# Opening a fused attention and MLP kernel head by head, with row sums in two parts and a fixed order of reciprocals

## The chip, the cores and the metric

One core of one Trainium2 chip. The metric is the device time of one execution in microseconds (us). The kernel before has a median of 1029.04 us over three runs, from 1028.91 to 1029.87.

## What is computed

An attention over 4 batches of 8 heads (576 positions, head size 64), then two MLPs over its 2304 rows. The scores carry a bias made of cumulative sums, which must be ready before the first scores can be formed:

```python
scores = scale * np.matmul(q, k.transpose(0, 1, 3, 2))
cum = np.cumsum(np.maximum(s, 0.0), axis=-1)
bias = -(cum[:, :, :, None] - cum[:, :, None, :])
scores = np.where(causal, -1e9, scores + np.minimum(bias, 0.0))
attn = exp(scores - max); attn = attn / (sum + 1e-9); out = attn @ v
h = x @ w_in;  x = (h * sigmoid(1.702 * h)) @ w_out          # d_model 512, d_ff 2048
h = x @ w2_in; x = (P(h) / Q(h)) @ w2_out                    # P cubic, Q quadratic
```

## The kernel before, in words

**Units.** The attention (`attention`, L401) walks through 16 pairs of heads, four to a batch, and through five blocks of query rows in each pair, in the order 0, 1, 4, 2, 3. So there are 80 units; step j of the loop at L422 forms the scores of unit j, transposes the weights of unit j-3 and multiplies those of unit j-4 by the values. Pair g holds units 5g to 5g+4, and its first scores stand at the start of step 5g.

**Operands of a pair.** Each float32 product is made from rounded high parts and remainders (low parts). `prep` (L170) transposes k and q on TensorE (`main`, L216), writes high parts on ScalarE and low parts on VectorE (`split`, L189), and copies two of them to other partitions (`move`, L227: on GpSimd for pairs 0 and 1, by a DMA on SyncE's queue for the others). Partitions 64 to 67 of the tile `k2` hold the bias: two rows of a sum's high and low part and two rows of ones, so that the matmul itself adds the difference of the sums (`scores_piece`, L248). `bias` (L204) fills these rows: for pair 0 by four DMAs from the sums on the chip (tile `stgA`) and two of ones; for a later pair by one DMA from a DRAM copy, `rows`, which `store_sums` (L112) writes with four DMAs on GpSimd's queue and four on SyncE's. The pair after next is loaded by `pair_load` (L141); k and q have one buffer each (L146), so a fetch of k waits until the transposes of the pair before it have read the buffer.

**Sums.** `sums` (L94) takes the maximum with 0, runs the scan over all 576 positions for all 32 heads, and splits the result into high and low parts.

**A unit's chain.** `unit_scores` (L263) runs per head: two matmuls (L258), a masked minimum on VectorE (L288), exp with a row sum on ScalarE (L295). Then once per unit: 1e-9 is added on GpSimd (L303), VectorE takes the reciprocal (L304), GpSimd scales the weights (L307). The transposes on TensorE (L328, L349) read the scaled weights; `unit_values` (L359) multiplies by v.

**What sets the order.** TensorE's order is the program's own. On the other engines and on the queues a planner orders the instructions within their dependencies. `behind` (L529) adds an edge: what is traced inside it, and runs on the engine of the given instruction, is put after that instruction; it adds no wait on another engine. Weights for the first MLP are loaded (L497, L499) into three slots of `stgA`, whose space the sums use first, and converted by `convert` (L502, on ScalarE, VectorE and GpSimd) at the steps of `CONV_J` (L52), the first at j = 9. Up to step 24 (`cold`) `fill` (L389) puts idle matmuls (L78, `warm`) into TensorE's stream; after it, matmuls of the first MLP.

Of the kernel before, what the change touches and what calls it, by code (L numbers as in the profile page):

```python
# [10 lines left out]
F32 = mybir.dt.float32  # L11
F32R = mybir.dt.float32r
# [3 lines left out]
AF = mybir.ActivationFunctionType  # L16
ALU = mybir.AluOpType
# [9 lines left out]
NP = NH // 2  # L27
NT = NB * S
DM, DF = 512, 2048
P = 128  # L30
# [15 lines left out]
AHEAD = 3  # L46
COPY_V = ((0, 0), (0, 4))
PT_W = (256, 512, 768, 1024)
RUN_ENDS = ((0, 1, 4, 2, 3), (4, 3), (4, 3), (3,))
W2_SLOTS = 7  # L50
LEAD = 2
# [7 lines left out]
class Fused:  # L59
    def __init__(self, tc, q, k, v, s, w1i, w1o, w2i, w2o, a, b, out):  # L60
        self.tc, self.nc = tc, tc.nc
        self.q, self.k, self.v, self.s = q, k, v, s
        self.w = {n: (i.bitcast(I32), o.bitcast(I32)) for n, i, o in ((1, w1i, w1o), (2, w2i, w2o))}
        self.a, self.b, self.out = a, b, out
        self.units = {}
        self.newest = {}


    def consts(self, pool):
# [24 lines left out]
    def sums(self, att):  # L94
        nc = self.nc
        BH = NB * NH
        s32 = self.s32
        nz = att.tile([BH, S], F32, name="nz", tag="bt", bufs=BT_BUFS)
        nc.vector.memset(nz, 0.0)
        self.rows = self.dram.tile([BH // 2, 4, 2, 2, S], F32, name="rows")  # L100
        part = self.stg_slot[:BH, : 6 * S].rearrange("p (i r s) -> p i r s", i=3, r=2)
        self.ones, self.hl = part[:, 0:2].bitcast(F32), part[:, 2]
        for i in range(2):
            nc.gpsimd.memset(self.ones[:, i], 1.0 - 2.0 * i)
        nc.vector.tensor_scalar(s32, s32, 0.0, None, ALU.max)
        cum = att.tile([BH, S], F32, name="cum", tag="bt", bufs=BT_BUFS)
        nc.vector.tensor_tensor_scan(cum, s32, nz, 0.0, ALU.add, ALU.add)
        hi, lo = (self.hl[:, r].bitcast(F32R) for r in range(2))
        nc.scalar.activation(hi, cum, AF.Copy)
        nc.vector.tensor_tensor(lo, cum, hi.bitcast(F32), ALU.subtract)  # L110

    def store_sums(self):  # L112
        nc = self.nc
        for i in range(2):
            for r in (2 * i, 2 * i + 1):
                nc.gpsimd.dma_start(self.rows[:, r, i], self.ones[:16, i])
            for h in range(2):
                nc.sync.dma_start(
                    self.rows[:, 2 - 2 * i : 4 - 2 * i, i, h],
                    self.hl[16 * h : 16 * h + 16].bitcast(F32),  # L120
                )


    def masks(self, att):
# [16 lines left out]
    def pair_load(self, att, b, p, first=False):  # L141
        nc = self.nc
        r = {"v": self.vn[p % 2]}

        for nm, src, eng in (("k", self.k, nc.sync), ("q", self.q, nc.scalar if first else nc.sync)):
            r[nm] = t = att.tile([R6, 2, 6, D], F32, name=f"{nm}n{b}_{p}", tag=f"{nm}n", bufs=1)  # L146
            for h in (slice(0, 1), slice(1, 2)) if first else (slice(0, 2),):
                eng.dma_start(
                    t[:, h].rearrange("i h t d -> i h (t d)"),
                    src[b, 2 * p : 2 * p + 2][h].rearrange("h (i t) d -> i h (t d)", t=6),  # L150
                )

        def values():
            if b == 0 and p < 2:
                nc.gpsimd.memset(r["v"][64:, 4], 0.0)
            if b == 0 and p == 0:
                nc.gpsimd.memset(self.pt4[64:, 512:], 0.0)
# [12 lines left out]
    def prep(self, att, b, p, ld, first=False):  # L170
        nc, ident = self.nc, self.ident
        h0, h1 = slice(0, D), slice(D, P)

        def new(nm, *n):
            return att.tile([P, *n, 2, S], F32R, name=f"{nm}{b}_{p}", tag=nm, bufs=2)

        kh, qs, k2 = new("kh"), new("qs"), new("k2", 2)
        self.pairs[b, p] = {"kh": kh, "qs": qs, "k2": k2, "ld": ld, "O": None}  # L180

        def hi(out, T, scale):
            nc.scalar.activation(out, T, AF.Copy, scale=scale)

        def lo(out, T, h, scale):
            nc.vector.scalar_tensor_tensor(out, T, scale, h.bitcast(F32), ALU.mult, ALU.subtract)


        def split(nm, T, h):  # L189
            T = T.rearrange("p (t i) -> p i t", i=R6)  # L190
            for odd, r in enumerate((h0, h1)):
                t = T[r]

                def cols(x):
                    return x.rearrange("p (i t o) -> p o i t", t=3, o=2)[:, odd]

                if nm == "k":
                    hi(cols(kh[h0, h]), t, 1.0)
                    lo(cols(k2[h0, 0, h]), t, cols(kh[h0, h]), 1.0)
                else:  # L200
                    hi(cols(qs[h0, h]), t, -0.125)
                    lo(cols(qs[h1, h]), t, cols(qs[h0, h]), -0.125)

        def bias():  # L204
            d = k2[D : D + 4].bitcast(F32)
            if not first:
                nc.sync.dma_start(d, self.rows[b * NP + p])
                return
            for i in range(2):
                nc.gpsimd.dma_start(d[2 * i : 2 * i + 2, i], self.ones[:2, i])  # L210
                for h in range(2):
                    nc.sync.dma_start(
                        d[2 - 2 * i : 4 - 2 * i, i, h], self.hl[16 * h : 16 * h + 1].bitcast(F32)
                    )

        def main(nm):  # L216
            for h in range(2):
# [9 lines left out]
        def move(o, i):  # L227
            if b == 0 and p < 2:
                for h in range(2):
                    nc.gpsimd.tensor_copy(o[:, h], i[:, h].bitcast(F32))  # L230
            else:
                nc.sync.dma_start(o.bitcast(F32), i.bitcast(F32))

        bias()
        if first:
            self.warm(4)
        main("k")
        move(kh[h1], kh[h0])
        yield
        if first:  # L240
            self.warm(4)
        main("q")
        move(k2[h0, 1], qs[h0])
        yield

# [17 lines left out]
    def unit_scores(self, att, u, h):  # L263
# [39 lines left out]
        nc.gpsimd.tensor_scalar(inv[:, c], sm[:, c], 1.0e-9, None, ALU.add)  # L303
        rc = nc.vector.reciprocal(inv[:, c], inv[:, c])  # L304
        self.tail = (ex, rc)
        for i, bt in enumerate(bts):
            nc.gpsimd.tensor_scalar(bt[:, :n], bt[:, :n], inv[:, i : i + 1], 1.0, ALU.mult, ALU.mult)  # L307

# [92 lines left out]
    def attention(self, att, mlp):  # L401
        units = [(b, p, t) for b in range(NB) for p in range(NP) for t in (0, 1, 4, 2, 3)]
        n = len(units)
        self.pairs, self.state = {}, {}
# [7 lines left out]
        self.pt4 = att.tile([P, 640], F32, name="pt4", bufs=1)  # L412
        ld = self.pair_load(att, 0, 0, True)
        self.sums(att)
        for _ in self.prep(att, 0, 0, ld, True):
            pass
        start = ld["values"]
        ld = self.pair_load(att, 0, 1)
        start()
        ld["values"]()  # L420
        self.store_sums()
        for j in range(n + AHEAD + 1):  # L422
            i, k = j - AHEAD, j - AHEAD - 1
            tr = iter(())
# [19 lines left out]
            self.fill(q / 3, j < 4)  # L444
            for _ in tr:
                pass
# [509 lines left out]
```

## Time and profile before

| | |
|---|---|
| median of three runs | 1029.04 us |
| the profiled execution: its time / its span | 1032.16 us / 1030.4 us |
| TensorE (PE) busy | 1008.7 us, 98% of the span |
| VectorE (DVE), ScalarE (ACT), GpSimd (POOL) busy | 77%, 70%, 33% |
| DMA read / written | 75.08 MB / 32.05 MB |
| mean granted TensorE clock | 0.993 of full speed |

The profile shows one execution. A row gives the engine, the line in the kernel, the operation, what it wrote and read, and its times. An engine with the letter q (SPq, ACTq, POOLq) is its instruction queue, where DMAs are issued; PEld is the loading of weights into TensorE. Names in the rows are the kernel's tiles: `kn`, `qn` and `vn` are k, q and v as loaded, `tk` and `tq` their transposes, `k` is the tile `k2`, `s` the scores in PSUM (and, on DVE at the start, the loaded s), `cum` the sums, `bt` the weights, `sm` the row sums, `tp` transposed weights, `O` the outputs.

### The profile page before, as it was taken

The numbers are of one execution on the slowest core, as the hardware profiler recorded it, in microseconds if no ns is written. First come the engines' busy times: TensorE is split into PE (matmuls) and PEld (weight loads), VectorE is DVE, ScalarE is ACT, GpSimd is POOL, SyncE is SP. The second block draws the span as 40 slices with busy tenths as digits, with TensorE's granted clock in tenths as the row PEclk, the third lists the DMA queues.
The fourth block names the chain that finished last, engine by engine and source line by source line (L and its number), as shares of the span: only waits on it lengthen the run. The fifth ranks groups of instructions, "written<-read, shape, count | busy, mean of one in ns | idle before, by whom it ended". The sixth has DMA issues, their size and how long they took to land.

```text
span 1030.4 us, 19824 instructions
## 1 busy us (share of the span) xinstructions
PE 1008.7 (98%) x7065; PEld 940.5 (91%) x7074; DVE 797.9 (77%) x1794; ACT 722.7 (70%) x1660; POOL 340.4 (33%) x512
## 2 busy tenths in 40 slices
PE   7999999999999999999999999999999999999997
PEld 4778899999999999999999999899999899999896
DVE  6698767766537977777777847899988989889886
ACT  5799979888756655555555536777877777777765
POOL 6478746644430002322211112222222222222222
PEclk9899999999999999999999999999999999999999
DMA  7366456454218645667657645010010100100000
GB/s 182 91 168 168 106 156 192 123 139 103 56 41 284 194 148 186 214 219 241 235 161 251 203 126 226 1 31 31 1 62 1 32 31 1 62 1 1 32 1 31
DMA packets 79594, 116.71 MB, mean 113 GB/s; under 512 B 25696, under 2 KB 63584, under 8 KB 77900
## 3 DMA queue, kind: packets, MB, share of 16 engines
q1 hardware_dynamic: 73128, 95.96, 31.4%
q0 software_dynamic: 6144, 19.19, 5.2%
q8 instruction: 56, 0.92, 0.4%
q10 hardware_dynamic: 224, 0.30, 0.1%
q14 instruction: 42, 0.34, 0.1%
HBM read 75.08 MB, written 32.05 MB: 104 GB/s over the span
## 4 chain that ended last, share of the span: by engine, by line
PE 89%; DMA 3%; ACT 3%; DVE 2%; issue 1%; POOL 1%; SPq 0%; ACTq 0%; POOLq 0%; DVEq 0%
PE h L585 37%; PE a L762 19%; PE a L609 18%; PE s L258 5%; PE O L374 4%; PE tp L349 3%; DMA raw<-in_moe_w_in_dram 1%; DMA kn<-in_k_dram 1%; ACT bt L295 1%; PE tk L221 1%; PE tp L328 1%; DMA x2p<-st 1%; PE tq L221 0%; DMA raw<-in_moe_w_out_dram 0%; PE idle L78 0%
## 5 line engine op out<-in xcount | busy, mean ns | idle before, releaser
L585 PE MATMUL h<-x,u 128*128 128x288 f32 x1536 | 231.8, 296 | 2.1 <-ACT st L624 1.1
L609 PE MATMUL a<-gh,u 128*128 128x288 f32 x1024 | 231.7, 297 | 0.0
L585 PEld LDWEIGHTS h<-x,u 128*128 128x128 f32 x1536 | 212.9, 188 | 4.5 <-ACT st L624 1.3
L745 POOL TENSOR_TENSOR gl<-u,gh 128x384 fp32r<-128x384 f32 x96 | 105.5, 1099 | 291.4 <-ACT gh L743 245.8
L609 PEld LDWEIGHTS a<-gh,u 128*128 128x128 f32 x1024 | 172.9, 188 | 1.4 <-issue 0.5
L585 PE MATMUL h<-y,u 128*128 128x384 f32 x864 | 165.7, 336 | 0.0
L585 PEld LDWEIGHTS h<-y,u 128*128 128x128 f32 x864 | 152.9, 188 | 6.2
L609 PE MATMUL a<-gl,u 128*128 128x288 f32 x512 | 150.0, 294 | 0.3 <-DVE gl L602 0.3
L762 PE MATMUL a<-u,gh 128*128 128x512 f32 x432 | 114.6, 394 | 0.9 <-ACT gh L743 0.9
L596 ACT ACTIVATE g<-h 128x288 f32<-128x288 f32 x128 | 52.2, 408 | 83.0 <-PE h L585 82.1
L671 POOL DMA_DIRECT2D x<-xp x64 | 35.3, 553 | 206.2 <-DVE g L597 89.4
L295 ACT ACTIVATE bt<-bt,mn 128x128 f32<-128x128 f32 (+2 forms) x144 | 83.6, 582 | 19.9 <-DVE mn L288 17.8
L609 PEld LDWEIGHTS a<-gl,u 128*128 128x128 f32 x512 | 96.5, 188 | 1.1 <-DVE gl L602 0.6
L762 PEld LDWEIGHTS a<-u,gh 128*128 128x128 f32 x432 | 80.0, 188 | 14.9 <-ACT gh L743 1.8
L288 DVE CUSTOM_DVE_ANT_0 bt<-s,mask 128x128 f32<-128x128 f32 (+2 forms) x144 | 69.2, 482 | 30.6 <-PE s L258 28.2
L307 POOL TENSOR_SCALAR bt<-bt,sm 128x128 f32<-128x128 f32 (+2 forms) x144 | 81.6, 577 | 29.0 <-DVE sm L304 20.7
L743 ACT ACTIVATE gh<-u 128x384 fp32r<-128x384 f32 x96 | 50.6, 527 | 55.0 <-DVE u L741 53.1
L599 ACT ACTIVATE gh<-g 128x288 fp32r<-128x288 f32 x128 | 56.4, 442 | 43.0 <-DVE g L597 41.5
L597 DVE SCALAR_TENSOR_TENSOR g<-g,h 128x288 f32<-128x288 f32 x128 | 57.5, 450 | 32.5 <-ACT g L596 31.4
L728 ACT ACTIVATE y<-h,cf 128x384 f32<-128x384 f32 x96 | 55.5, 578 | 37.6 <-PE h L585 37.6
L258 PE MATMUL s<-k 68*128 68x256 f32 (+2 forms) x192 | 72.4, 382 | 4.3 <-DMA k<-stgA 3.8
L733 DVE SCALAR_TENSOR_TENSOR y<-s,cf,y 128x384 f32<-128x384 f32 x96 | 59.3, 618 | 21.7 <-ACT s L730 20.7
(109 smaller groups left out, 2071.9 us busy)
## 6 DMA issues: line engine op xcount, KB each, us to landing
raw<-in_moe_w_in_dram SPq DMA_DIRECT2D x24, 512.0 KB
raw<-in_moe_w_out_dram SPq DMA_DIRECT2D x24, 512.0 KB
x<-xp POOLq DMA_DIRECT2D x64, 144.0 KB, 2.9
wd<-park POOLq DMA_DIRECT2D x36, 256.0 KB, 3.8
u<-wd SPq DMA_DIRECT2D x8, 1024.0 KB
x2p<-st SPq DMA_DIRECT2D x32, 144.0 KB
xp<-x2p SPq DMA_DIRECT2D x32, 144.0 KB
xp<-x SPq DMA_DIRECT2D x32, 144.0 KB
```

What stands on the lines that cost most here:

```text
L258: nc.tensor.matmul(sc[: c1 - c0, :w], lhsT=q[:, c0:c1], rhs=k[:, j0 : j0 + w], start=m == 0, stop=m == 1,)
L288: nc.vector.tensor_tensor_reduce(bt[:, j0 : j0 + w], sc[:, :w], mask, 1.0, 3.0e38 if i == 0 else mn[:, 0:1], ALU.add, ALU.min, mn[:, i : i ...
L295: ex = nc.scalar.activation(bt[:, :n], bt[:, :n], AF.Exp, bias=mn[:, i : i + 1], scale=-1.0, accum_out=sm[:, col : col + 1],)
L307: nc.gpsimd.tensor_scalar(bt[:, :n], bt[:, :n], inv[:, i : i + 1], 1.0, ALU.mult, ALU.mult)
L585: nc.tensor.matmul(ps_tile, lhsT=u[:, wl, kk * P : (kk + 1) * P], rhs=x(xl, kk), start=(n == 0), stop=(n == 3 * KD - 1),)
L597: nc.vector.scalar_tensor_tensor(g[:, :w], g[:, :w], 1.0, h, ALU.add, ALU.mult)
L599: self.newest["act"] = nc.scalar.activation(gh[:, :w], g[:, :w], AF.Copy)
L609: nc.tensor.matmul(acc, lhsT=u[:, wl, d * P : (d + 1) * P], rhs=g[gl], start=(first and i == 0), stop=(last and i == 2),)
L728: nc.scalar.activation(y, h, AF.Abs, scale=cf[:, 4:5])
L733: nc.vector.scalar_tensor_tensor(y, s, cf[:, 7:8], y, ALU.mult, ALU.add)
L745: nc.gpsimd.tensor_tensor(gl, p, gh.bitcast(F32), ALU.subtract)
L762: nc.tensor.matmul(accs[m], lhsT=g[gl][:, m * P : (m + 1) * P], rhs=u[:, wl, :], start=(f == 0 and i == 0), stop=(f == NF - 1 and i == 2),)
```

## The change

It touches the attention's opening and some orders:

- `sums` works in two parts, positions 0 to 255 and 256 to 575.
- Two lasting tiles take the place of the `k2` tiles allotted per pair. Their partitions 64 to 67 are set to 1 or -1 once, by VectorE for one and GpSimd for the other; later only the rows of sums are overwritten (`sum_rows`). `rows` in DRAM holds the sums alone: two DMAs write it in place of eight, and two in place of one read it per pair.
- Pair 0 is prepared head by head (k and q of head 0, then of head 1), with 8, 7 and 4 idle matmuls in place of 10, 4 and 4. Its rows of sums come by eight DMAs (part, head, kind of row) on SyncE's queue.
- Pair 1's rows come from the sums on the chip by four DMAs on GpSimd's queue, behind the copies of pair 0, not from DRAM.
- Pair 0's values and the store of the sums stand behind pair 0's rows and pair 1's fetch of q on SyncE's queue; pair 1's values are asked for at step 2.
- The loads of weights at the steps of `CONV_J` and `AHEAD_J` stand behind the newest fetch of q on SyncE's queue.
- `split` writes both high parts, then both low parts.
- In batch 0, VectorE's work on the scores of a unit's first head stands behind the reciprocal of the unit two before, that of its second head, and that of `prep`, behind the reciprocal of the unit before (`guard`).

```diff
+PARTS = ((0, 256), (256, 576))
@@ sums
-        self.rows = self.dram.tile([BH // 2, 4, 2, 2, S], F32, name="rows")
-        for i in range(2):
-            nc.gpsimd.memset(self.ones[:, i], 1.0 - 2.0 * i)
-        nc.vector.tensor_scalar(s32, s32, 0.0, None, ALU.max)
-        nc.vector.tensor_tensor_scan(cum, s32, nz, 0.0, ALU.add, ALU.add)
...
+        self.rows = self.dram.tile([BH // 2, 2, 2, S], F32, name="rows")
+        self.hl = self.stg_slot[:BH, 4 * S : 6 * S].rearrange("p (r s) -> p r s", r=2)
+        self.k2 = [att.tile([P, 2, 2, S], F32R, name=f"k2_{i}", bufs=1) for i in range(2)]
+        for k2, eng in zip(self.k2, (nc.vector, nc.gpsimd)):
+            for i in range(2):
+                eng.memset(k2[D : D + 4, i].bitcast(F32), 1.0 - 2.0 * i)
+        for c0, c1 in PARTS:
+            c = slice(c0, c1)
+            with self.behind((scan,) if c0 else ()):
+                nc.vector.tensor_scalar(s32[:, c], s32[:, c], 0.0, None, ALU.max)
+            scan = nc.vector.tensor_tensor_scan(
+                cum[:, c], s32[:, c], nz[:, c], cum[:, c0 - 1 : c0] if c0 else 0.0, ALU.add, ALU.add
+            )
+            hi, lo = (self.hl[:, r, c].bitcast(F32R) for r in range(2))
+            nc.scalar.activation(hi, cum[:, c], AF.Copy)
+            nc.vector.tensor_tensor(lo, cum[:, c], hi.bitcast(F32), ALU.subtract)
+    def store_sums(self):
+        for h in range(2):
+            self.nc.sync.dma_start(self.rows[:, :, h], self.hl[16 * h : 16 * h + 16].bitcast(F32))
+    def sum_rows(self, g, src, eng, h=slice(0, 2), c=slice(0, S)):
+        d = self.k2[g % 2][D : D + 4].bitcast(F32)
+        for i in range(2):
+            self.rows_in = eng.dma_start(d[2 - 2 * i : 4 - 2 * i, i, h, c], src)
@@ prep
+            for t, o in zip((T[h0], T[h1]), cols(high)):
+                hi(o, t, scale)
+            for t, o, i in zip((T[h0], T[h1]), cols(low), cols(high)):
+                lo(o, t, i, scale)
...
+            for h in range(2):
+                with self.behind(tuple(self.parts) if h else ()):
+                    main("k", (h,))
+                    main("q", (h,))
+                move(kh[h1], kh[h0], (h,))
+                move(k2[h0, 1], qs[h0], (h,))
+                self.warm(4 if h else 7)
+            return
+        if g > 1:
+            self.sum_rows(g, self.rows[g], nc.sync)
@@ unit_scores
+        self.guard = (rc,) if b == 0 else (), self.guard[0]
@@ attention
-        self.warm(10)
+        self.warm(8)
...
+        for c0, c1 in PARTS:
+            for h in range(2):
+                self.sum_rows(0, self.hl[16 * h : 16 * h + 1, :, c0:c1].bitcast(F32), nc.sync,
+                              h, slice(c0, c1))
+        rows = self.rows_in
...
+        with self.behind((self.moved,)):
+            for h in range(2):
+                self.sum_rows(1, self.hl[16 * h + 1 : 16 * h + 2].bitcast(F32), nc.gpsimd, h)
+        with self.behind((rows, self.fetched)):
+            start()
+            self.store_sums()
+        later.append(ld["values"])
...
-                self.unit_scores(att, units[j], 0)
+                with self.behind(self.guard[1]):
+                    self.unit_scores(att, units[j], 0)
                 if j:
-                    next(nprep, None)
+                    with self.behind(self.guard[0]):
+                        next(nprep, None)
+                if j == 2:
+                    with self.behind((rows, self.fetched)):
+                        later.pop(0)()
...
-                self.unit_scores(att, units[j], 1)
+                with self.behind(self.guard[0]):
+                    self.unit_scores(att, units[j], 1)
...
             if j in CONV_J or j in AHEAD_J:
-                with self.behind(self.tail):
+                with self.behind((*self.tail, self.fetched)):
                     self.emit(1)
```

## Rows read from the trace of the kernel before

**Rows 1.** The page: the span in 40 equal slices, in tenths.
```profile
PE   7999999999999999999999999999999999999997
PEclk9899999999999999999999999999999999999999
```

**Rows 2.** Windows by pair: length; PE, PEld, DVE, ACT, POOL busy; clock, DMA share, GB/s.
```profile
12.00:25.15 13.15, 10.79 (x58) 7.73 (x60) 8.53 (x32) 8.76 (x25) 6.15 (x15) 0.87 0.80 222
25.15:43.50 18.35, 17.09 (x126) 13.60 (x126) 10.91 (x40) 11.79 (x33) 6.23 (x15) 0.72 0.34 83
43.50:58.00 14.50, 13.23 (x127) 10.30 (x127) 12.71 (x45) 13.99 (x40) 9.24 (x16) 1.00 0.53 143
58.00:72.00 14.00, 13.72 (x126) 10.48 (x129) 12.38 (x44) 13.74 (x40) 11.21 (x18) 1.00 0.71 180
```

**Rows 3.** The chain of waits, 0 to 30 us: start, length, what.
```profile
4.00 0.46 DVE s L105
4.49 1.36 DVE cum L107
5.87 0.69 ACT stgA L109
6.58 0.75 DVE stgA L110
...
8.80 3.06 DMA k<-stgA
...
16.97 9.52 DMA kn<-in_k_dram
```

**Rows 4.** The timeline of SyncE's queue, 0 to 30 us: start, length, what.
```profile
7.36 2.62 SPq L212 DMA_DIRECT2D k<-stgA  x4
10.08 0.36 SPq L148 DMA_DIRECT2D kn<-in_k_dram  x1
...
11.40 1.95 SPq L118 DMA_DIRECT2D rows<-stgA  x4
13.53 0.39 SPq L497 DMA_DIRECT2D stgA<-in_moe_w_in_dram  x1
...
15.99 0.93 SPq L497 DMA_DIRECT2D stgA<-in_moe_w_in_dram  x2
16.97 0.50 SPq L148 DMA_DIRECT2D kn<-in_k_dram  x1
```

**Rows 5.** The timeline of TensorE, 0 to 46 us, with the idle time before.
```profile
11.99 0.55 PE L258 MATMUL s<-k 68*128 68x256 f32 x1 [3.81 <-DMA k<-stgA]
...
14.74 0.95 PE L221 MATMUL tk<-ident,kn 96*128 96x96 f32 x6
...
23.48 0.89 PE L349 MATMUL tp<-ident,bt 128*128 128x128 f32 x4 [2.34 <-POOL bt L307]
...
25.15 0.39 PE L258 MATMUL s<-k 68*128 68x256 f32 x1
...
26.63 1.19 PE L221 MATMUL tk<-ident,kn 96*128 96x96 f32 x6 [0.97 <-DMA kn<-in_k_dram]
...
43.54 0.39 PE L258 MATMUL s<-k 68*128 68x256 f32 x1
```

**Rows 6.** The timeline of GpSimd, 0 to 52 us: start, length, what.
```profile
8.55 0.99 POOL L116 DMA_DIRECT2D rows<-stgA  x2
...
10.92 1.27 POOL L230 CAST k<-qs 64x576 fp32r<-64x576 f32 x2
...
18.63 0.22 POOL L303 TENSOR_SCALAR sm<-sm 128x2 f32<-128x2 f32 x1
...
22.95 0.94 POOL L307 TENSOR_SCALAR bt<-bt,sm 128x256 f32<-128x256 f32 x2 [1.47 <-DVE sm L304]
...
49.04 1.30 POOL L515 TENSOR_TENSOR stgA<-stgA 128x512 int32<-128x512 int32 x1
```

**Rows 7.** The timeline of VectorE, 20 to 52 us: start, length, what.
```profile
22.69 0.16 DVE L304 RECIPROCAL sm<-sm 128x2 f32<-128x2 f32 x1
```

More of the change, by code (lines that the diff above doesn't have):

```diff
@@ L66, in __init__ @@
         self.newest = {}
+        self.parts = [None, None]
+        self.guard = (), ()
     def consts(self, pool):
@@ L99, in sums @@
         nc.vector.memset(nz, 0.0)
-        self.rows = self.dram.tile([BH // 2, 4, 2, 2, S], F32, name="rows")
-        part = self.stg_slot[:BH, : 6 * S].rearrange("p (i r s) -> p i r s", i=3, r=2)
-        self.ones, self.hl = part[:, 0:2].bitcast(F32), part[:, 2]
-        for i in range(2):
-            nc.gpsimd.memset(self.ones[:, i], 1.0 - 2.0 * i)
-        nc.vector.tensor_scalar(s32, s32, 0.0, None, ALU.max)
-        cum = att.tile([BH, S], F32, name="cum", tag="bt", bufs=BT_BUFS)
-        nc.vector.tensor_tensor_scan(cum, s32, nz, 0.0, ALU.add, ALU.add)
@@ L108, in sums @@
[L108 to L113, printed above, removed]
-        for i in range(2):
[L115 to L121, printed above, removed]
+        self.rows = self.dram.tile([BH // 2, 2, 2, S], F32, name="rows")
@@ new lines, in sums @@
+        self.hl = self.stg_slot[:BH, 4 * S : 6 * S].rearrange("p (r s) -> p r s", r=2)
[3 more added lines that the diff above has]
+                eng.memset(k2[D : D + 4, i].bitcast(F32), 1.0 - 2.0 * i)
+        cum = att.tile([BH, S], F32, name="cum", tag="bt", bufs=BT_BUFS)
+        for c0, c1 in PARTS:
[8 more added lines that the diff above has]
+            nc.vector.tensor_tensor(lo, cum[:, c], hi.bitcast(F32), ALU.subtract)
@@ L124, in masks @@
+    def store_sums(self):
+        for h in range(2):
+            self.nc.sync.dma_start(
+                self.rows[:, :, h], self.hl[16 * h : 16 * h + 16].bitcast(F32)
+            )
+    def sum_rows(self, g, src, eng, h=slice(0, 2), c=slice(0, S)):
+        d = self.k2[g % 2][D : D + 4].bitcast(F32)
+        for i in range(2):
+            self.rows_in = eng.dma_start(d[2 - 2 * i : 4 - 2 * i, i, h, c], src)
     def masks(self, att):
@@ L147, in pair_load @@
             for h in (slice(0, 1), slice(1, 2)) if first else (slice(0, 2),):
-                eng.dma_start(
+                self.fetched = eng.dma_start(
                     t[:, h].rearrange("i h t d -> i h (t d)"),
@@ L153, in values @@
         def values():
[L154 to L157, printed above, removed]
             for h in range(2):
@@ L172, in prep, with new @@
         h0, h1 = slice(0, D), slice(D, P)
-        def new(nm, *n):
-            return att.tile([P, *n, 2, S], F32R, name=f"{nm}{b}_{p}", tag=nm, bufs=2)
-        kh, qs, k2 = new("kh"), new("qs"), new("k2", 2)
+        def new(nm):
+            return att.tile([P, 2, S], F32R, name=f"{nm}{b}_{p}", tag=nm, bufs=2)
+        g = b * NP + p
+        kh, qs, k2 = new("kh"), new("qs"), self.k2[g % 2]
         self.pairs[b, p] = {"kh": kh, "qs": qs, "k2": k2, "ld": ld, "O": None}
         def hi(out, T, scale):
-            nc.scalar.activation(out, T, AF.Copy, scale=scale)
+            self.parts[0] = nc.scalar.activation(out, T, AF.Copy, scale=scale)
@@ L185, in lo @@
         def lo(out, T, h, scale):
-            nc.vector.scalar_tensor_tensor(out, T, scale, h.bitcast(F32), ALU.mult, ALU.subtract)
+            self.parts[1] = nc.vector.scalar_tensor_tensor(
+                out, T, scale, h.bitcast(F32), ALU.mult, ALU.subtract
+            )
         def split(nm, T, h):
             T = T.rearrange("p (t i) -> p i t", i=R6)
[L191 to L217, printed above, removed]
+            scale = 1.0 if nm == "k" else -0.125
@@ L218, in main, with cols @@
+            high, low = (kh[h0, h], k2[h0, 0, h]) if nm == "k" else (qs[h0, h], qs[h1, h])
+            def cols(x):
+                x = x.rearrange("p (i t o) -> p o i t", t=3, o=2)
+                return x[:, 0], x[:, 1]
+            for t, o in zip((T[h0], T[h1]), cols(high)):
+                hi(o, t, scale)
+            for t, o, i in zip((T[h0], T[h1]), cols(low), cols(high)):
+                lo(o, t, i, scale)
+        def main(nm, hs=(0, 1)):
+            for h in hs:
                 T = self.bank("T", f"t{nm}{b}_{p}_{h}")
@@ L224, in main, with move @@
                 split(nm, T[:, : 3 * R6], h)
[L227 to L230, printed above, removed]
+        def move(o, i, hs=(0, 1)):
+            if g < 2:
+                for h in hs:
+                    self.moved = nc.gpsimd.tensor_copy(o[:, h], i[:, h].bitcast(F32))
             else:
                 nc.sync.dma_start(o.bitcast(F32), i.bitcast(F32))
-        bias()
         if first:
-            self.warm(4)
+            for h in range(2):
[8 more added lines that the diff above has]
+            self.sum_rows(g, self.rows[g], nc.sync)
         main("k")
@@ L239, in prep @@
         yield
-        if first:
-            self.warm(4)
         main("q")
@@ L403, in attention @@
         n = len(units)
+        nc = self.nc
         self.pairs, self.state = {}, {}
@@ L412, in attention @@
         self.pt4 = att.tile([P, 640], F32, name="pt4", bufs=1)
+        for t in (*(v[64:, 4] for v in self.vn), self.pt4[64:, 512:]):
+            nc.gpsimd.memset(t, 0.0)
         ld = self.pair_load(att, 0, 0, True)
         self.sums(att)
+        for c0, c1 in PARTS:
+            for h in range(2):
+                self.sum_rows(
+                    0, self.hl[16 * h : 16 * h + 1, :, c0:c1].bitcast(F32), nc.sync,
+                    h, slice(c0, c1),
+                )
+        rows = self.rows_in
         for _ in self.prep(att, 0, 0, ld, True):
@@ L418, in attention @@
         ld = self.pair_load(att, 0, 1)
-        start()
-        ld["values"]()
-        self.store_sums()
+        with self.behind((self.moved,)):
+            for h in range(2):
+                self.sum_rows(
+                    1, self.hl[16 * h + 1 : 16 * h + 2].bitcast(F32), nc.gpsimd, h
+                )
+        with self.behind((rows, self.fetched)):
+            start()
+            self.store_sums()
+        later.append(ld["values"])
         for j in range(n + AHEAD + 1):
```

## Prediction

> **What bounds the kernel now.** I read four views in this order. First the page's slices: TensorE is at nine tenths or more in all slices but the first and the last [rows 1], and its granted clock is at full speed but for the second slice. A gain must therefore come from the start, where TensorE still waits, and it lasts to the end if nothing between gives it back: TensorE's order is fixed, so all that is behind moves up. Second, windows by pair [rows 2]. Pairs 2 and 3 take 14.50 and 14.00 us with ScalarE busy for 13.99 and 13.74: ScalarE bounds them. Pair 1 takes 18.35 with ScalarE busy for 11.79 only and a mean clock of 0.72; the same matmuls (126 instructions against 127) keep TensorE busy for 17.09 against 13.23 us in pair 2, which has the full 2.4 GHz. Half of pair 1 runs at the lower level, 1.2 GHz. Pair 0, at 13.15, has neither VectorE (8.53) nor ScalarE (8.76) full.
>
> Third, the chain of waits names what holds these two pairs [rows 3]: the sums, one after another on VectorE and ScalarE; the DMA that carries them into pair 0's operand (3.06 us, the first scores at 11.99 wait for it); and then 9.52 us of a fetch of k. That is pair 2's, issued at 16.97 [rows 4] and used at 26.63 [rows 5]. Ahead of it in SyncE's queue stand three loads of weights of 512 KB, from 13.53 and 15.99, though the first conversion that reads them comes with unit 9. Fourth, TensorE's timeline [rows 5]: besides 3.81 us ahead of the first scores it idles 2.34 us at 23.48 for unit 1's weights, and 0.97 at 26.63. Behind the 2.34 lies an order: GpSimd has unit 1's sums ready at 18.63 + 0.22 = 18.85 [rows 6], VectorE takes the reciprocal at 22.69 [rows 7]. The clock fell after these idle stretches.
>
> **The opening.** Before, from 4.00 to 7.33 the sums take 0.46, 1.36, 0.69 and 0.75 us for 576 columns [rows 3]. No row shows a part of 256 columns: by columns it is 0.20, 0.60, 0.31 and 0.33, 1.44 in all; at worst each part costs as much as the whole, 3.3. I take 1.9, nearer the share, with some 0.1 for each instruction: the first part is out at 5.9. SyncE issues the four row DMAs at 2.62 / 4 = 0.65 each [rows 4]. Two serve head 0's first part: issued by 7.2, landed 3.06 later, 10.3. Two more serve head 1: 11.6. Scores started at 11.99 for both heads' rows. Head 0 gains 1.6, head 1 some 0.4; since unit 0 ends with head 1 but VectorE and ScalarE start with head 0, I take **1.2**, between 0 (parts cost as much as the whole) and 2.5 (rows land faster, since pair 0's and 1's values no longer stand ahead of them). GpSimd is no gate: it loses its issues of ones and `rows` (four times 0.99 / 2 [rows 6]) and so can copy when ScalarE delivers; it gains four issues for pair 1 of some 0.5, behind those copies. They lie in its idle time before unit 0's sums; if not, 0.5 us. Setting the lasting rows to 1 falls on VectorE and GpSimd before s arrives at 4.00; GpSimd did as much before. No row shows it on VectorE: between 0 and 1 us, I take 0, as s is not there earlier.
>
> The four row DMAs that are added put pair 1's fetch of k at 5.9 + 8 * 0.65 = 11.1 in place of 10.08, landing by the same 3.06 at 14.5 (with its issue of 0.36), when TensorE wanted it at 14.74 before [rows 5] and would now want it earlier. So TensorE may wait a little in unit 1. I charge **0.5**, between 0 and 1.2 (the whole gain ahead of it). The stores of `rows` shrink from 1.95 on SyncE to half and from two issue pairs on GpSimd to none; each later pair needs one more read of `rows`. SyncE has room for both: nothing.
>
> Here a rule speaks against the change. Rows 3 and 4 show four transfers issued in 2.62 us, all landed 4.5 us after the first issue (7.36 to 11.86); so they overlap, and eight end about 2.6 us later than four. The Trainium skill, DMA: Bandwidth & Descriptors, "Rules for kernel authors", says to merge many small transfers, as below 64 KB one pays mostly overhead, and its "Anatomy of one DMA" gives a fixed cost of about 2.0 us to each. If that were paid one after another, an estimate from that page is 16 us for the eight, the last landing near 22, and the sum would be some 1029. The rows decide for overlap.
>
> **Pair 0.** The reciprocal of unit 1 now stands ahead of what VectorE does for later units. It can follow at 18.9; GpSimd may have a copy of 1.27 in front and then scales in 0.94 [rows 6], so the weights are there by 21.2 in place of 23.48: the 2.34 goes. What is late next is VectorE: it now waits in order for exp and GpSimd, with pair 1's low parts and the next minima queued behind the reciprocal, and ScalarE waits for those. Its share of 8.53 in 13.15 leaves that room. I take **1.8**, between 0.5 and 2.3.
>
> **Pair 1.** The three loads are put behind pair 3's fetch of q. Without 1.5 MB in front, at the window's 222 GB/s some 6.9 us [rows 2], pair 2's fetch lands in about 9.52 - 6.9 = 2.6 us, near 19 to 20, and is there when wanted. The 0.97 goes, and with idle stretches gone the clock stays at its upper level: 17.09 - 13.23 = 3.9 us less of TensorE. That is 13.5 us for 18.35; ScalarE's 11.79 is the floor. I take 14.0, **4.3** less; at least 1.0 (the wait alone, the clock falls again), at most 5.4.
>
> **Pairs 2 to 5.** ScalarE bounds them, and its work does not change: 0 gained. Two things may cost. Two of the moved loads (1 MB, 4.7 us at that rate) now run after pair 2's transposes, near 26 us, beside the DMAs that copy pair 2's operands; these have some 8 us until pair 2's scores: nothing, at most 1.5. And VectorE behind a reciprocal waits for GpSimd, where a conversion puts two operations of 1.30 [rows 6] in front of a unit's sums: up to 2.6 us at each of the four conversions of batch 0 (steps 9, 12, 15, 18), 10.4 in all. VectorE idles 1.8 and 1.6 us in pairs 2 and 3, which takes up most of it. I charge **0.8**, between 0 and 10.4.
>
> **Sum.** 1.2 - 0.5 + 1.8 + 4.3 - 0.8 = 6.0 us. The profiled execution took 1032.16 us over a span of 1030.4, 3.1 above the median; its span would be 1024.4, and from the median 1029.04 - 6.0 = **1023.0**.
>
> **Rivals.**
> *The clock falls again.* TensorE still idles in pair 0 (pair 1's k late, weights late) and pair 1 runs half at 1.2 GHz. For it: pair 0 has TensorE doing 10.79 of 13.15 us even with slow matmuls in it. Against: the two longest waits have named causes, and both go. Gain 1.2 - 0.5 + 1.5 + 1.0 - 0.2 = 3.0: 1026.0.
> *It is given back.* The weights come later by some 13 us; if the first conversions wait for them, or the copies of pair 2 do, all behind keeps its old time: 1029.0. Against: two loads end near 31 and unit 9 is worked on near 36.
> *Small transfers end one after another*: by rows 3, 8 * 3.06 = 24 us for the eight if each had to land before the next. The blocks that need the second part would start after 26; the rest of the gain is lost: about 1029 or above. Rows 4 speaks against it; the skill's rule on small transfers is what speaks for it.
> *Slower: VectorE waits for reciprocals.* Place: the minima at L288 behind L304 in batch 0, from step 9. Price: 10.4, not covered, against the 6.8 gained: 1029.04 - 6.8 + 10.4 = 1032.6. It decides once the uncovered waits pass 6.8 us. Against: VectorE's idle time in these pairs, and GpSimd's order is the planner's, which need not put a conversion first.
>
> **How the numbers follow.** Forecast 0.58; clock falls again 0.24; given back 0.08; small transfers 0.02; slower 0.08. A run can tell about 0.2%, 2.06 us, from no change. Faster by more: 0.58 + 0.24 = 0.82; within: 0.10; slower: 0.08. The range takes in the first two cases (0.82): from 1020.0, with the opening at 2.5, nothing charged for row DMAs and pair 1 near its floor (1029.04 - 2.5 - 1.8 - 4.7), to 1027.0, the second case with another 1.0 lost.
>
> **What would show it.** Right: the first scores at 10 to 11 us; loads of weights after pair 3's fetch of q on SyncE's queue; pair 2's fetch landing within 4 us; no wait over 1 us at the transposes of unit 1; a window of about 14 us for pair 1 at a clock near 1.0; pair 2's first scores near 37.5 in place of 43.54, and the same difference kept at 72 us and at the end. Wrong: a clock under 0.8 in pair 1 (second case); pair 2's first scores early, but TensorE waiting for weights after them; or ScalarE idle in pairs 2 and 3 with VectorE waiting at L304.

## The result, and the profile after

The changed kernel takes 1040.25 us (median of 6 runs, 1036.39 to 1040.96) against 1028.97 for the kernel before (1027.93 to 1030.61). The ratio is 1.0100, with a 95% interval from 1.0088 to 1.0112: 11.3 us slower, where I had forecast 6.0 faster and a range up to 1027.0. The profiled execution took 1040.53 over a span of 1038.3.

The page's slices of the changed kernel stand first. The clock is now below nine tenths in the first, the second and the fourth slice, where before it was so in the second alone [rows 1].

```profile
PE   7898999999999999999999999999999999999997
PEclk8898999999999999999999999999999999999999
```

The windows by pair have the columns of [rows 2]: length; busy us of TensorE, its weight loads, VectorE, ScalarE, GpSimd; clock, DMA. Each starts near the first scores of pairs 0 to 4. The last row is of the kernel before, for pair 4, which [rows 2] leaves out.

```profile
12.00:25.41 13.41, 9.67 (x52) 6.90 (x52) 6.29 (x22) 5.59 (x17) 5.51 (x12) 0.75 0.61 144
25.41:44.50 19.09, 16.94 (x119) 13.09 (x121) 11.75 (x44) 13.83 (x39) 7.19 (x17) 0.73 0.47 123
44.50:59.00 14.50, 13.48 (x128) 10.40 (x128) 12.44 (x44) 14.10 (x38) 9.25 (x15) 1.00 0.70 178
59.00:76.00 17.00, 15.16 (x127) 11.52 (x127) 13.16 (x46) 14.12 (x39) 10.23 (x18) 0.90 0.48 124
76.00:98.00 22.00, 17.23 (x141) 13.55 (x141) 16.67 (x52) 20.41 (x53) 14.51 (x22) 0.92 0.55 149
...
72.00:89.00 17.00, 14.82 (x134) 11.92 (x135) 14.84 (x50) 16.03 (x45) 14.20 (x22) 1.00 0.60 163
```

Pair 1 is no shorter than the 18.35 of before and no better clocked. Pair 3 has grown from 14.00 to 17.00, and every engine is busy for a smaller share of it: something waits there that did not. Pair 4 has grown from 17.00 to 22.00. The timeline of SyncE's queue (start, length, what) shows the opening, to be read against [rows 4].

```profile
7.02 5.07 SPq L130 DMA_DIRECT2D k<-stgA  x8
12.19 0.35 SPq L157 DMA_DIRECT2D kn<-in_k_dram  x1
...
18.21 0.53 SPq L157 DMA_DIRECT2D kn<-in_k_dram  x1
...
32.40 1.01 SPq L521 DMA_DIRECT2D stgA<-in_moe_w_in_dram  x2
```

TensorE's timeline answers [rows 5]; the bracket gives the idle time before and what ended it.

```profile
9.60 0.36 PE L259 MATMUL s<-k 68*128 68x256 f32 x1 [0.78 <-DMA k<-stgA]
...
15.77 1.20 PE L216 MATMUL tk<-ident,kn 96*128 96x96 f32 x6 [3.37 <-DMA kn<-in_k_dram]
...
23.51 0.89 PE L351 MATMUL tp<-ident,bt 128*128 128x128 f32 x4
...
25.76 0.66 PE L216 MATMUL tk<-ident,kn 96*128 96x96 f32 x6
```

The first scores come 2.4 us earlier (11.99 before). Then TensorE waits 3.37 us for pair 1's k, which SyncE could issue only at 12.19, behind eight row DMAs, and which landed 3.45 us later. Pair 2's fetch, issued at 18.21, is there when it is wanted at 25.76, without the 0.97 of before. But unit 1's weights are transposed at 23.51, as before (23.48). The timelines of GpSimd and VectorE, which answer [rows 6, 7], say why:

```profile
22.47 0.22 POOL L304 TENSOR_SCALAR sm<-sm 128x2 f32<-128x2 f32 x1
22.98 0.94 POOL L309 TENSOR_SCALAR bt<-bt,sm 128x256 f32<-128x256 f32 x2 [0.29 <-DVE sm L305]
```
```profile
17.89 0.93 DVE L192 SCALAR_TENSOR_TENSOR k<-tk,kh 64x288 fp32r<-64x288 f32 x2 [4.62 <-ACT kh L189]
...
22.72 0.17 DVE L305 RECIPROCAL sm<-sm 128x2 f32<-128x2 f32 x1 [0.17 <-POOL sm L304]
```

The reciprocal now follows GpSimd's sum at once, in place of 3.84 us later. But the sum itself is as late as the reciprocal was. Unit 1's second scores stand behind the transposes of pair 1's k, and VectorE idles 4.62 us for the same fetch. That is not all of it, though. ScalarE writes pair 1's four high parts of q before the exp that the sum needs; in e1, a run described below whose fetch is as late but which lacks the order of the reciprocals, the exp comes first and GpSimd's sum at 20.31. The two rows of the changed kernel, and then the exp and the sum of e1:

```profile
19.86 1.79 ACT L189 ACTIVATE qs<-tq 64x288 fp32r<-64x288 f32 x4 [1.10 <-PE tq L216]
21.54 0.49 ACT L296 ACTIVATE bt<-bt,mn 128x256 f32<-128x256 f32 x1
...
19.23 0.51 ACT L296 ACTIVATE bt<-bt,mn 128x256 f32<-128x256 f32 x1 [0.55 <-DVE mn L289]
20.31 0.21 POOL L304 TENSOR_SCALAR sm<-sm 128x2 f32<-128x2 f32 x1
```

Where pair 3 ends and pair 4 begins there is a second wait. One timeline of all engines:

```profile
78.04 0.36 PE L259 MATMUL s<-k 68*128 68x256 f32 x1
...
80.53 0.71 ACT L296 ACTIVATE bt<-bt,mn 128x512 f32<-128x512 f32 x1
...
81.42 0.21 POOL L304 TENSOR_SCALAR sm<-sm 128x2 f32<-128x2 f32 x1 [2.10 <-DMA kn<-in_k_dram]
...
81.67 0.17 DVE L305 RECIPROCAL sm<-sm 128x2 f32<-128x2 f32 x1 [0.86 <-POOL sm L304]
...
81.75 1.87 DVE L192 SCALAR_TENSOR_TENSOR k<-tk,kh 64x288 fp32r<-64x288 f32 x4
...
82.80 0.52 PE L351 MATMUL tp<-ident,bt 128*128 128x128 f32 x3 [2.48 <-DVE k L192]
...
83.65 0.29 DVE L289 CUSTOM_DVE_ANT_0 bt<-s,mask 128x128 f32<-128x128 f32 x1
```

Read it from the bottom. The minimum of unit 20's second head begins at 83.65, though its scores began at 78.04. It stands behind a burst of four low parts, and these stand, by the new order, behind the reciprocal of unit 19 at 81.67. That waits for GpSimd and so for an exp that ScalarE reaches at 80.53. (The releaser that the row at 81.42 names is the fetch of another pair's k; GpSimd reads row sums there, so the exp is what it needs.) TensorE's transposes at 82.80 read weights and a constant, not k; they wait 2.48 us for a low part because, as I read the code, the attention's eight PSUM buffers go round, and the next one is the one that the transpose of k still holds. After it the clock drops: 0.92 over this window, where the kernel before has 1.00.

How it adds up shows in the start of the first transpose of k of some pairs, in us, from the profiled executions (e3 and e6 are, like e1, runs described below):

| pair | before | changed | e1 | e3 | e6 |
|---|---|---|---|---|---|
| 1 | 14.74 | 15.77 | 15.69 | 13.00 | 13.41 |
| 2 | 26.63 | 25.76 | 27.82 | 22.57 | 23.42 |
| 3 | 43.88 | 45.83 | 41.86 | 39.81 | 37.50 |
| 5 | 72.03 | 76.97 | 70.50 | 69.38 | 66.08 |
| 6 | 89.73 | 99.15 | 89.69 | 91.72 | 83.82 |
| 7 | 110.57 | 119.81 | 110.71 | 112.20 | 104.69 |
| 15 | 263.11 | 271.66 | 264.39 | 264.15 | 257.26 |

Against the kernel before, the changed kernel loses 2.8 us from pair 2 to pair 3, 3.0 up to pair 5 and 4.5 up to pair 6, and keeps most of it: 8.55 at pair 15, 7.9 in the span.

The first of these understates, since the kernel before was slow there itself (17.25 us). Against e1, which lacks the order of the reciprocals, the changed kernel is 2.1 us ahead at pair 2, then loses 6.0 from pair 2 to pair 3, 2.5 up to pair 5 and 3.0 up to pair 6. From pair 2 to pair 3 it takes 20.07 us at a clock of 0.74, e1 14.04 at 1.00, and e3, which has the order but an early fetch, 17.24 at 1.00. So by these executions the order costs some 3 us there by waits alone, and some 3 more where the clock falls too. What brings the clock down is not shown: there TensorE waits 1.04, 0.57 and 0.48 us in the changed kernel, and 1.04, 0.56 and 1.29 in e3, whose clock stays up. The windows of the changed kernel, e1 and e3:

```profile
25.76:45.83 20.07, 17.92 (x127) 13.53 (x127) 12.69 (x48) 14.55 (x41) 7.99 (x19) 0.74 0.48 124
...
27.82:41.86 14.04, 13.48 (x128) 10.24 (x127) 10.91 (x41) 12.09 (x34) 7.02 (x17) 1.00 0.69 182
...
22.57:39.81 17.24, 14.00 (x128) 10.15 (x127) 12.81 (x48) 14.43 (x41) 8.00 (x19) 1.00 0.56 149
```

### The profile page after: what moved, and what is told of

It is laid out like the page before. It is cut to its first block, busy times and chain, and to the rows that moved or that the text cites. A ratio compares the mean times of both kernels' runs of the same rounds, so it can differ in the third digit from the quotient of the medians.

```text
span 1038.3 us, 19882 instructions
## 1 busy us (share of the span) xinstructions
PE 1014.7 (98%) x7066; PEld 944.6 (91%) x7075; DVE 800.7 (77%) x1799; ACT 728.9 (70%) x1661; POOL 340.6 (33%) x510
## 4 chain that ended last, share of the span: by engine, by line
PE 89%; DVE 4%; DMA 3%; ACT 2%; issue 1%; POOL 1%; SPq 0%; ACTq 0%; POOLq 0%; DVEq 0%
PE h L609 37%; PE a L786 19%; PE a L633 18%; PE s L259 6%; PE O L376 4%; PE tp L351 3%; DMA raw<-in_moe_w_in_dram 1%; DVE k L192 1%; DMA kn<-in_k_dram 1%; PE tk L216 1%; DMA x2p<-st 1%; PE tp L330 1%; DVE qs L192 1%; PE tq L216 0%; ACT bt L296 0%
```

## The experiments

Three theories. G: the order of the reciprocals costs. K: the late fetch of pair 1's k, and the low clock behind it, cost. W: the weights, loaded later, delay their conversions. A ratio is to the kernel before, timed beside the run; prices in us are differences of medians. The changed kernel's 1040.25 comes from a set of runs of its own; between the sets, the medians of the kernel before lie within 0.65 us.

**e1, without the order of the reciprocals.**

```diff
-        self.guard = (rc,) if b == 0 else (), self.guard[0]
```

> The changed kernel without the order of the reciprocals (nothing stands behind the reciprocal of an earlier unit). Theory G (the order costs: low parts and minima queue behind a reciprocal, and the low parts hold PSUM banks that the transposes want): 1027 to 1032, TensorE waits no more for DVE at the transposes, but pair 1's k is still late by over 3 us. Theory K (the 3.4 us wait for pair 1's k and the low clock after it are the loss): 1037 to 1041, as before the edit. Theory W (weights loaded late delay the conversions): 1037 to 1041.

Measured: 1032.93 us, ratio to the kernel before 1.0031 (1.0018 to 1.0044). So 7.3 us of the loss are G's. The fetch is late as before the edit:

```profile
15.69 1.19 PE L216 MATMUL tk<-ident,kn 96*128 96x96 f32 x6 [2.69 <-DMA kn<-in_k_dram]
```

This lies just above the 1027 to 1032 that I expected of G; something is left.

**e2, the order of the reciprocals alone, on the kernel before.** 
```diff
+        self.guard = (rc,) if b == 0 else (), self.guard[0]
...
+                with self.behind(self.guard[1]):
+                    self.unit_scores(att, units[j], 0)
                 if j:
+                    with self.behind(self.guard[0]):
+                        next(nprep, None)
...
+                with self.behind(self.guard[0]):
+                    self.unit_scores(att, units[j], 1)
```

> The kernel before with that order alone added. G: 1034 to 1041, with waits of TensorE for DVE k at the transposes near the start of a pair, as in the changed kernel. K and W: 1027 to 1031, since neither the row DMAs nor the loads of weights are touched.

Measured: 1034.74, ratio 1.0051 (1.0035 to 1.0066). The order costs about 5.5 us with nothing else changed. K and W fall as sole causes.

**e3, pair 1's fetch ahead of the second part's rows.**

```diff
-        for c0, c1 in PARTS:
-            part_rows(c0, c1)
+        part_rows(*PARTS[0])
...
         ld = self.pair_load(att, 0, 1)
+        with self.behind((self.fetched,)):
+            part_rows(*PARTS[1])
```

(`part_rows` stands for the loop over the two heads.)

> The changed kernel with pair 1's fetches of k and q put ahead of the four row DMAs of the second part on SyncE's queue; nothing else. K: the fetch is issued near 9.7 in place of 12.19, the wait for it falls from 3.4 us to about 1, the clock in the first two pairs rises, 1033 to 1037. G and W: 1038 to 1041; the gain is eaten at the next reciprocal.

Measured: 1034.26, ratio 1.0047 (1.0025 to 1.0070): 6.0 us less, as K had it. No wait for pair 1's k is left; its transposes start at 13.00, 2.8 us earlier. Its runs lie apart: four take 1032.65 to 1034.26 at a mean clock of 0.994 or 0.995, three 1037.4 to 1037.7 at 0.988 to 0.990. By the four the price is 6.0 to 7.6 us, by the three 2.5 to 2.8. The profiled execution is one of the four; what sets the three apart is not shown.

**e4, weights early again.**

```diff
-                with self.behind((*self.tail, self.fetched)):
+                with self.behind(self.tail):
```

> The changed kernel without the edge that puts loads of weights behind the newest fetch of q. W: 1028 to 1034. G and K: 1038 to 1043; the loads again stand in front of pair 2's fetch of k, so slower by up to 2 us if anything.

Measured: 1039.65, ratio 1.0090 (1.0059 to 1.0122). W falls.

**e5, both edits of e1 and e3, as their diffs show them.**

> The changed kernel with both edits: no order of the reciprocals, and pair 1's fetch ahead of the second part's row DMAs. If the two causes are separate and add (1040.3 - 7.3 - 6.0): 1026 to 1028, faster than the kernel before. If both edits free the same waiting time: 1031 to 1033.

Measured: 1029.42, ratio 1.0006 (0.9997 to 1.0015), between my two ranges. The two do not quite add: of 7.3 and 6.0 together 10.8 are gained. And the kernel is still not faster than the one before, though its first scores are. TensorE's timeline points to a third cause, in pairs 5 to 7, where no reciprocal is in any order:

```profile
84.47 1.33 PE L612 MATMUL h<-x,u 128*128 128x288 f32 x8 [1.96 <-DVE x L386]
...
90.35 0.47 PE L216 MATMUL tq<-ident,qn 96*128 96x96 f32 x3 [0.95 <-DVE k L192]
...
112.06 0.44 PE L216 MATMUL tq<-ident,qn 96*128 96x96 f32 x3 [1.08 <-DVE k L192]
```

**e6, as e5, and the split goes high, low, high, low again.**

```diff
-            for t, o in zip((T[h0], T[h1]), cols(high)):
-                hi(o, t, scale)
-            for t, o, i in zip((T[h0], T[h1]), cols(low), cols(high)):
-                lo(o, t, i, scale)
+            for t, o, l in zip((T[h0], T[h1]), cols(high), cols(low)):
+                hi(o, t, scale)
+                lo(l, t, o, scale)
```

> As the run with both edits, and the split again writes high, low, high, low. Theory S (both high parts first hold the PSUM bank of a transpose longer, and TensorE waits for it from pair 4 on): 1 to 3 us under the run with both edits. If the order of the split is nothing: within 1 us of it.

Measured: 1025.69 (1025.09 to 1027.63), ratio 0.9972 (0.9962 to 0.9983). It is 3.7 us under e5, more than the 1 to 3 of my theory, and beats both kernels. The same places in its timeline:

```profile
82.40 1.33 PE L611 MATMUL h<-x,u 128*128 128x288 f32 x8 [0.42 <-DVE x L385]
...
109.00 0.47 PE L215 MATMUL tq<-ident,qn 96*128 96x96 f32 x3 [0.51 <-DVE mn L288]
```

The 1.96 is down to 0.42 and the waits for DVE k are gone. The 1.96 is a wait for data, since these matmuls read x, which VectorE writes; only the waits for DVE k can be waits for a PSUM buffer. Two windows (the columns are as above) show the clock back at full from 26 us on; from pair 2's to pair 3's transposes it takes 37.50 - 23.42 = 14.08 us.

```profile
12.00:26.00 14.00, 13.15 (x82) 9.51 (x81) 9.92 (x37) 10.37 (x32) 9.84 (x22) 0.88 0.55 131
26.00:44.00 18.00, 16.06 (x160) 12.32 (x161) 14.89 (x54) 15.42 (x47) 8.07 (x18) 1.00 0.69 184
```

**e7, late weights alone, on the kernel before.** `self.fetched` is set by the fetch as in the changed kernel.

```diff
-                with self.behind(self.tail):
+                with self.behind((*self.tail, self.fetched)):
```

> The kernel before, with only the loads of weights put behind the newest fetch of q. My prediction's step (pair 2's fetch of k no longer behind 1.5 MB): that fetch lands within 4 us of its issue, pair 1 takes 14 to 16 us in place of 18.35, 1025 to 1027. Theory W (loads late): 1030 or above, with TensorE waiting for conversions from pair 4 on. If the clock stays low in pair 1 for the other waits: 1028 to 1029.

Measured: 1028.40, ratio 0.9993 (0.9984 to 1.0002): nothing. Its profiled execution does what I had predicted, though: no wait for pair 2's k, from pair 2's to pair 3's transposes 39.32 - 25.33 = 14.0 us in place of 17.25, a span of 1026.3, 4.1 under the profiled execution of before. The two statements meet when the runs of before are looked at. Of its 70 runs beside e1 to e12 the median is 1028.7, and three reach 1032 or more; the profiled execution, 1032.16, is of that kind. By the mean clock of a run: 23 runs at 0.997 have a median of 1028.0, 15 at 0.994 one of 1029.8, four at 0.993 one of 1032.4. The profiled execution is at 0.993. So it seems that what e7 saves was in that execution and is not in most; no other execution of the kernel before was profiled, so that is inferred.

**e8 and e9, the halves of the order, on the kernel before:** each is e2 with a part taken out. In e8 only `next(nprep)` stands behind the reciprocal, in e9 only the two calls of `unit_scores`. Against e2, e9 is

```diff
-                    with self.behind(self.guard[0]):
-                        next(nprep, None)
+                    next(nprep, None)
```

and e8

```diff
-                with self.behind(self.guard[1]):
-                    self.unit_scores(att, units[j], 0)
+                self.unit_scores(att, units[j], 0)
...
-                with self.behind(self.guard[0]):
-                    self.unit_scores(att, units[j], 1)
+                self.unit_scores(att, units[j], 1)
```

> The kernel before with the order of the reciprocals on the low parts of prep alone; the minima are free. If the low parts behind a reciprocal are the cost (they hold the banks of tk and tq): 1033 to 1035, near the 1034.7 of the whole order. If the minima behind a reciprocal are the cost: 1029 to 1031.

> The kernel before with the order of the reciprocals on the minima of both heads alone; prep's low parts are free. If the two halves of the order add up (whole: +5.5, prep alone: +1.8): 1032 to 1033. If only both together hurt, since burst and minima line up behind one reciprocal: 1028 to 1030.

Measured: e8 1030.36, ratio 1.0021 (1.0011 to 1.0031), in the range that I gave for the minima as the cost; e9 1031.21, ratio 1.0022 (1.0012 to 1.0032), which lies between its two ranges. Each half costs about 2 us (1.8 and 2.6 by the medians), the whole 5.5, somewhat more than both. Neither the low parts nor the minima are the only place.

**e10, the new order of the split alone, on the kernel before** (the lines that e6 takes out, put in the place of the old ones).

```diff
-            for odd, r in enumerate((h0, h1)):
...
+            for t, o in zip((T[h0], T[h1]), cols(high)):
+                hi(o, t, scale)
+            for t, o, i in zip((T[h0], T[h1]), cols(low), cols(high)):
+                lo(o, t, i, scale)
```

> The kernel before with the split in the new order alone (both high parts, then both low parts). If the order of the split costs by itself what it cost on top of the two edits (3.7 us): 1031 to 1033, with TensorE waiting for DVE k near 88 to 115 us. If it costs only through the planner's other choices in the changed kernel: 1028 to 1029.5.

Measured: 1033.02, ratio 1.0035 (1.0023 to 1.0047), 4.4 us by the medians and 3.6 by the ratio. The waits are those of e5; the last row is the first one's place in the kernel before:

```profile
87.67 1.34 PE L584 MATMUL h<-x,u 128*128 128x288 f32 x8 [1.96 <-DVE x L384]
...
115.49 0.44 PE L220 MATMUL tq<-ident,qn 96*128 96x96 f32 x3 [1.08 <-DVE k L186]
...
88.31 1.34 PE L585 MATMUL h<-x,u 128*128 128x288 f32 x8 [0.42 <-DVE x L385]
```

**e11, the changed kernel with the old split alone:** the diff of e6, without those of e1 and e3.

> The changed kernel with the old order of the split alone. If the three costs add: 1040.3 - 3.7 = 1036.6, from 1035.5 to 1038. If the reciprocals already set the order of the low parts, so that the split's order does nothing here: 1039 to 1041.

Measured: 1034.70, ratio 1.0055 (1.0042 to 1.0068): 5.5 us less than the changed kernel (4.6 by the ratios), more than the 3.7 that adding would give, and just under my range.

**e12, as e6, but the opening pair keeps the new split.** Against e6:

```diff
-            for t, o, l in zip((T[h0], T[h1]), cols(high), cols(low)):
+            pairs = list(zip((T[h0], T[h1]), cols(high), cols(low)))
+            for t, o, l in pairs:
                 hi(o, t, scale)
-                lo(l, t, o, scale)
+                if not first:
+                    lo(l, t, o, scale)
+            if first:
+                for t, o, l in pairs:
+                    lo(l, t, o, scale)
```

> As the version with all three edits, but the opening pair keeps both high parts first, and only later pairs go high, low, high, low. The second head's first scores then start near 10.8 in place of 11.8: 1024.5 to 1025.5 if that head is on the path, 1025.7 as before the edit if the second part's rows or pair 1's fetch end later anyway.

Measured: 1026.01 (1024.72 to 1027.90), ratio 0.9971 (0.9960 to 0.9983): not told apart from e6. The edit did what it was meant to: the second head's first scores, at 11.81 in e6, come at 10.81 (first row e6, second e12). The opening's second head is not what limits.

```profile
11.81 0.39 PE L258 MATMUL s<-k 68*128 68x256 f32 x1 [1.41 <-POOL k L224]
...
10.81 0.35 PE L263 MATMUL s<-k 68*128 68x256 f32 x1 [0.50 <-DMA k<-stgA]
```

So the loss has three causes, each shown by taking it out of the changed kernel and, for two of them, by putting it alone into the kernel before: the order of the reciprocals (7.3 out, 5.5 in), the late fetch of pair 1's k (6.0 out by the median of runs that lie apart), the split with both high parts first (5.5 out, 4.4 in). All three out, 14.6 us are gone and the rest of the change, with pair 1's fetch moved forward, is worth 2.9 us. What is not settled: that it is a PSUM buffer that TensorE waits for in the rows with DVE k is read from the code and the rows; no run gave it more of them. How much of each price is the wait and how much the clock that falls after it was not separated. And the planner chooses anew with each edit, so a share of each price is its choice.

## Why the prediction was wrong, step by step

Four steps failed. Pair 1's fetch, charged with 0.5, cost 6.0. The wait for reciprocals, charged with 0.8, cost 5.5 to 7.3. The order of the split, for which the sum has no term, cost 3.7 to 5.5. And pair 1's gain of 4.3 was 0.15 by the medians of e7. The sign that I had set for the second case was there too, a clock under 0.8 in pair 1 (0.73); but that case still had a gain of 3.0.

**The opening** was right in its mechanism: first scores at 9.60, where I had 10.3, and the wait for pair 0's rows down from 3.81 to 0.78. That the time is so near is partly luck. The first part's sums left at 7.0, not 5.9, and from there to the scores it took 2.6 us, not 4.4; the two errors nearly cancel. Eight row DMAs took 5.07 us of issue (0.65 each expected, 5.2). They overlapped: head 0's scores ran at 9.60, while the queue was still issuing until 12.09. The Trainium skill, DMA: Bandwidth & Descriptors, "Rules for kernel authors", says to merge small transfers, as under 64 KB one pays mostly overhead. The 2 us each that I took from its "Anatomy of one DMA" stand there for DMAs issued on GpSimd, and these eight go by SyncE's queue. They are not paid in a row here: head 1's first scores, which need four of the DMAs, ran at 10.81, 3.8 us after the first issue at 7.02. What did cost was the issue: 5.07 us of SyncE's queue, with the fetch of pair 1's k behind it.

**The 0.5 charged for pair 1's fetch** failed, and its upper bound of 1.2 with it. The issue came at 12.19, not 11.1, since the first part's sums left 1.1 us later than I had (the last section has the rows); it landed 3.45 us later. The wait was 3.37 and, by e3, worth 6.0. The bound was wrong in kind: I took "the whole gain ahead of it" as the most that could be lost, but behind this wait stood unit 1's second scores, VectorE (idle 4.62) and the clock, which stayed at half for the next matmuls (1.20 us for six transposes, as in the row at 26.63 of [rows 5]; at full clock, at 25.76, the same six take 0.66).

**Pair 0, 1.8 for the reciprocal**, was right where it is compared with the same kernel without the order. In e1 the reciprocal of unit 1 comes at 25.02, 4.5 us after its sums are ready (3.84 in the kernel before), and TensorE waits for the weights:

```profile
25.02 0.17 DVE L305 RECIPROCAL sm<-sm 128x2 f32<-128x2 f32 x1
...
25.82 0.90 PE L350 MATMUL tp<-ident,bt 128*128 128x128 f32 x4 [1.10 <-POOL bt L308]
```

With the order that wait is gone (23.51 in the changed kernel), and pair 2's transposes start at 25.76 against 27.82, 2.1 us earlier; with the early fetch they start at 22.57 with the order (e3) and at 24.02 without it (e5), 1.5 earlier. These are single executions. The gain was lost again at once, from pair 2 to pair 3, where the order costs more than it had brought.

**Pair 1, 4.3.** The mechanism was right in e6 and e7: without the weights in front pair 2's k is there, the clock stays up and the pair takes 14.1 and 14.0 us, where I had 14.0. In the changed kernel pair 2's k was there as well, but the clock fell. It did not in e1, which has the late fetch of pair 1 and lacks the order of the reciprocals: there the pair takes 14.04 us at a clock of 1.00. And the term was mis-sized: it was taken from an execution 3.1 us above the median, and I set the 3.1 aside as an offset that both kernels would carry. It seems to have been the very time I meant to save: e7 gives 4.1 us between the profiled executions and 0.15 between the medians. The same stands behind e6: 1032.16 - 1026.16 = 6.0 between the profiled executions and 2.9 between the medians. That 6.0 is also my sum is a coincidence and bears nothing out.

**Pairs 2 to 5, 0.8 charged with a bound of 10.4.** This is where the rival "VectorE waits for reciprocals" lay, and it came true: 5.5 alone, 7.3 in the changed kernel. Where the rows show it, it did so by another chain than mine. I had GpSimd's conversions in front of the sums, from step 9 on; at 81.67 the reciprocal waits for an exp of ScalarE, and from pair 2 to pair 3, where the order costs most, no conversion had begun. I let VectorE's idle 1.8 and 1.6 us per pair pay for the waits [rows 2]. Idle time pays only where it lies: here the waits fell at the start of a pair, where four low parts and the next minima come together behind one reciprocal, and TensorE needs the low parts' buffers. The largest loss against e1 is the 6.0 from pair 2 to pair 3; 3.0 are lost at unit 20, past batch 0, since the first steps of pair 4 still stand behind reciprocals of units 18 and 19. I gave this rival 0.08.

**The order of the split** has no step in the prediction at all. I listed the edit in the change and costed it at nothing without naming its cover. It is worth 3.7 to 5.5 us, and by e12 none of it is seen in the opening. Between the profiled executions of e5 and e6 most of it falls from pair 5's to pair 6's transposes (19.18 us against 17.74) and from pair 7's to pair 8's (22.68 against 21.52).

## What to carry to other kernels

An order that puts one engine's short instruction ahead of its next work makes all that work wait for the chain in front of that instruction; count who waits for the queued work, the buffers it would free included. A new wait is bounded by what stands behind it, not by the gain ahead of it. An edit that is listed in the change needs its own term in the sum. And where the profiled execution lies above the median, ask whether the time above it is the time one means to save, before it goes into the sum.

## What the runs showed of the hardware that I had not expected

One run of the same kernel has a clock that another has not: the kernel before takes from 1027.5 us at a mean clock of 0.997 to 1032.9 at 0.993, with no edit between them, and e3 from 1032.7 at 0.994 to 1037.7 at 0.990.

VectorE's first work on a part of the sums was slow. In the chain of waits of the changed kernel the maximum over 256 columns took 0.78 us where 576 had taken 0.46 [rows 3], while a memset of GpSimd ran (2.60 to 4.65 us); 320 columns right after took 0.29. VectorE also put the second scan ahead of the first part's low half, and the first part's sums left at 7.0, where I had 5.9. The rows, from the chain of waits (start, length, what):

```profile
2.98 0.89 DVE k L108
4.03 0.78 DVE s L113
4.83 0.72 DVE cum L114
```

The timelines of GpSimd fit two engines that take turns. In the changed kernel the maximum ends at 4.81, 0.16 us after the memset (first row below). In the kernel before, VectorE's maximum came first (4.00 to 4.46), and of two equal memsets of GpSimd the one that began beside it took 0.45 us, the other 0.20 (second and third row).

```profile
2.60 2.05 POOL L108 MEMSET k<- 4x1152 f32 x2
...
4.15 0.45 POOL L155 MEMSET vn<- 64x128 f32 x1
...
4.70 0.20 POOL L155 MEMSET vn<- 64x128 f32 x1
```

That the two engines hold each other up there is not shown: no run moved one of the two.
